# The product x^T k of the last eight tiles in two column halves, with a new order of the work around it

## The chip, the cores and the metric

The kernel runs on one core of a Trainium2 chip. The metric is the device time of one execution in microseconds (us); lower is better. The core has five engines with a queue of instructions each: TensorE (PE; its weight loads are listed as PEld), VectorE (DVE), ScalarE (ACT), GpSimd (POOL) and SyncE (SP), which here issues nearly all DMAs. An engine executes its own queue in order; engines wait for each other and for DMAs through semaphores.

## The reference

Two residual blocks on x (2048 rows of 512, bf16). The first is linear attention with 32 heads of 16 columns after a layernorm, the second a gated mixer; of the second only its outline matters here.

```
xn  = layernorm(x)
q, k, v = xn @ wqkv                      # 512 columns each, 32 heads of 16
phi(t) = where(t > 0, t + 1, exp(t)) + 1e-6
kv  = phi(k)^T v        per head         # 16 x 16
z   = sum over rows of phi(k)            # per head
o   = (phi(q) @ kv) / (phi(q) . z + 1e-6)
h   = x + o @ wo
y   = gelu(layernorm(h) @ w_in);  z1, z2 = halves of y;  z2 = layernorm(z2)
out = h + (z1 * (w_sp @ z2 + b_sp)) @ w_out
```

## The kernel before, in words

The 2048 rows are 16 tiles of 128 rows, in four groups of four tiles. The kernel does not form v. It sums x^T k, a 512 x 512 product of the normalised rows with phi(k), over the 16 tiles in PSUM, and then multiplies this sum by the columns of wqkv that belong to v, head block by head block, masks it to the heads, and multiplies it by wo: the result `mw` turns phi(q), divided by its denominator, straight into o @ wo.

`build` (line 400) writes every operation down once, with `op(engine, cost, function, r=..., w=..., want=..., name=...)`. `Program.schedule` (line 151) then puts the operations of each engine in an order: of those that are possible, it takes on each engine the one with the smallest sum of its planned start and half its `want`. The `want` values that count stand in the list `WANT` (line 359), in the order of the calls of `op` and in tenths of a planned us; they overwrite those of the calls at line 1103. `Program.waits` turns the data dependences into semaphore waits. So the order of each queue, SP's DMAs included, is fixed when the program is built, from planned times, and does not react to real ones.

The operations that the change and the prediction speak of, by name:

- `st`, `ag`, `rs`, `xn` (lines 590 to 668): layernorm of a tile; for tile n, `xn{n}` writes the normalised rows.
- `tx{n}` (line 675, called at 695 and 704): a DMA transpose on SP's queue which writes the transposed tile to `xT`; tiles 2 and 3 are transposed on PE instead, and for k tiles 0 and 1 too.
- `k{n}` (line 758): four matmuls of 512 columns. It needs `tx{n}`. Then `phi` (line 706) makes phi(k): exp by ACT, a `min` by DVE, a `relu` by ACT, and the `sum` by DVE. From tile 4 on, two tiles share these four. `phi` has a second form, used for q: instead of relu and sum, DVE alone does a `max` from PSUM (line 727).
- `xk{n}` (line 768): four matmuls of 512 columns which add the tile's x^T k to the tile `HT` in PSUM, four banks of the eight.
- `q{group}.{f}` (line 860): four matmuls of 512 columns, in pairs, with the group's phi behind them. They need all four transposes of the group.
- `zs`, `zrow`, `ztr`, `zw` (lines 780 to 793): the sum z. `den{group}` (line 873): the denominators of a group; then ACT's `ln` and `rd` (lines 877, 880) give the reciprocals, four DMAs on SP spread them (`sp{group}`, line 886), and DVE multiplies them into phi(q) (`sc{group}.{half}`, line 892).
- `hs{h}.{b}` (lines 801, 804): four copies of `HT` to SBUF, by column half h, one of ACT and one of DVE for each half. `kvT` (line 813), `kvm` (822), `mw` (829) and `mwc` (836, 839) lead from there to `mw`; `kvT1`, `mw1` need half h = 1, `kvT0`, `mw0` half h = 0.
- `o{n}` (lines 905, 912) and `h` (line 924): phi(q) times `mw`, and the residual by DVE. Then the second block: `z2` (968), `z1` (1023), `mix` (1063) and `out` (1083).
- `load` (line 538, the DMA is line 540): `wk`, `wq`, `wv`, `wo`, `win` and the rows of x. `wsp{group}.{st}` (line 1043): 64 DMA transposes from HBM for the mixer, on the same SP queue. `mix` of group 2 waits for all 16 of `wsp2`.

Two lines say how the order is chosen and how x^T k is summed:

```
key = (t + self.WEIGHT * o.want, o.seq)            # WEIGHT = 0.5
i = e.matmul(HT(bank(j)).ap(), lhsT=xn[n, j * P:(j + 1) * P].ap(), rhs=pk[n, :].ap(), ...
```

Of the kernel before, what the change touches and what calls it, by code (L numbers as in the profile page):

```python
# [10 lines left out]
P = 128  # L11
# [81 lines left out]
class Program:  # L93
# [263 lines left out]

UNIT = 0.1
WANT = [
# [37 lines left out]
]  # L397


def build(nc, A_x, A_wqkv, A_wo, B_w_in, B_w_sp, B_b_sp, B_w_out, out):  # L400
# [17 lines left out]
    LN1 = [[0], [1], [2, 3], [4, 5, 6, 7], [8, 9, 10, 11], [12, 13, 14, 15]]  # L418
    LN2 = [[0, 1], [2, 3], [4, 5], [6, 7], [8, 9, 10, 11], [12, 13, 14, 15]]
    ACT_RELU_K = set(range(0, 16))  # L420
    ACT_RELU_Q = set()
    ACT_NORM1 = {5, 7, 9, 11, 13, 15}
    ACT_NORM2 = set()
    ACT_Z = {1, 2, 3, 5, 6, 7, 9, 10, 11, 13, 14, 15}
    UNIT_RES = set()
    FIRST_O = 2

    x_dram, out_dram = A_x[0], out[0]
    g = Program(nc)
# [142 lines left out]
    op("act", (0.1, 1.3), lambda e: e.preload_act_table_set("natural_log_exp_and_others"), want=-40, name="table")  # L572


    HT = Tile(PS, 4)

    def filler(e):
        return e.matmul(HT(bank(0)).ap(), lhsT=nc.const_aps.tensor(1.0, [P, P], BF16),  # L578
                        rhs=nc.const_aps.tensor(1.0, [P, GW], BF16), start=True, stop=True)

    def spin(e):
        for _ in range(SPIN):
            i = filler(e)
        return i
    op("pe", (SPIN * 0.43, SPIN * 0.43 + 0.2), spin, w=[HT()], want=-60, name="spin")
    g.filler = filler


# [148 lines left out]
    for un in UNITS:  # L737
        w = len(un)
        t = Tile(PS, w)
        for ti, n in enumerate(un):  # L740
            lhs = xcT[n].all() if n in LATE else xT[:, n * P:(n + 1) * P]
            for h in range(2):
                rhs = wqkv[2 * h:2 * h + 2, D:2 * D]

                def mm(e, t=t, ti=ti, lhs=lhs, rhs=rhs, h=h):
                    for c in range(2):
                        i = e.matmul(t(bank(ti)).ap(), lhsT=lhs.ap()[:, 2 * h + c, :], rhs=rhs.ap()[:, c, :],
                                     start=(h == 0 and c == 0), stop=(h == 1 and c == 1))
                    return i
                if n in LATE:  # L750
                    op("pe", pe_c(512, 512), mm, r=[xcT[n][2 * h:2 * h + 2, :], rhs, cT[n]()], w=[t()], want=T1(n),
                       name=f"k{n}.{h}")
            if n not in LATE:
                rhs = wqkv[:, D:2 * D]

                def mm(e, t=t, ti=ti, lhs=lhs, rhs=rhs):
                    for c in range(KD):
                        i = e.matmul(t(bank(ti)).ap(), lhsT=lhs.ap()[:, c, :], rhs=rhs.ap()[:, c, :], start=(c == 0),  # L758
                                     stop=(c == KD - 1))
                    return i  # L760
                op("pe", pe_c(*[512] * 4), mm, r=[lhs, rhs], w=[t()], want=T1(n), name=f"k{n}")
        d = pk[un[0]:un[-1] + 1, :]
        src = (lambda t: t(flat).ap()) if w == 2 else (lambda t: t(bank(0)).ap())
        phi(t, w, d, src, False, un[0] in ACT_RELU_K, rs1[un[0]] if un[0] in LATE else None, T1(un[0]) + 1, f"pk{un[0]}")
        for n in un:
            def xk(e, n=n):
                for j in range(KD):
                    i = e.matmul(HT(bank(j)).ap(), lhsT=xn[n, j * P:(j + 1) * P].ap(), rhs=pk[n, :].ap(),  # L768
                                 start=(n == 0), stop=(n == NT - 1))
                return i  # L770
            op("pe", pe_c(*[512] * 4), xk, r=[xn[n, :], pk[n, :]], w=[HT()], want=T1(n) + 3, name=f"xk{n}")


    T0 = T1(NT) + 3
# [21 lines left out]
    for h in range(2):  # L796
        for b in range(2):
            d = hs[2 * b:2 * b + 2, 2 * h * P:2 * (h + 1) * P]
            src = HT(lambda a, b=b, h=h: a[:, 2 * b:2 * b + 2, 2 * h * P:2 * (h + 1) * P])
            if b == 0:  # L800
                op("act", act_c(512), lambda e, d=d, src=src: e.activation(d.ap(), src.ap(), ACT.Copy), r=[HT()], w=[d],
                   want=T0 + 0.5 + h, name=f"hs{h}.0")
            else:
                op("dve", dve_c(512), lambda e, d=d, src=src: e.tensor_copy(d.ap(), src.ap()), r=[HT()], w=[d],
                   want=T0 + 0.5 + h, name=f"hs{h}.1")
    for b in range(2):
        kt, t = Tile(PS), Tile(PS, 2)
# [381 lines left out]
```

## Time and profile before

| | us |
|---|---|
| three runs, median | 241.91 |
| three runs, lowest and highest | 241.69, 244.42 |
| the profiled execution, its own time | 242.55 |
| its span, first to last instruction | 240.8 |
| PE busy in the span | 235.3 |
| DVE, ACT, POOL busy | 127.1, 83.9, 13.9 |

The span is the time between the first and the last instruction that the profiler recorded; the execution's own time is 1.75 us more. A timeline row gives the start, the length in which its merged instructions were busy, the engine (SPq is SP's queue, which issues DMAs), the line, the operation, what it writes and reads, the count, and in brackets how long the engine was idle before. PE's multiplies overlap, so a timeline row of PE ends about 0.17 us after the next one has begun; start to start is the better measure, and the chain of waits shows it. A row "to landing" gives the time from a DMA's issue to its completion.

### The profile page before, as it was taken

Reading aid. Unit: us, or ns where it says so; the run is one execution under the profiler, and the core shown is the slowest. Engines: PE = TensorE matmul, PEld = TensorE weight load, DVE = VectorE, ACT = ScalarE, POOL = GpSimd, SP = SyncE. Lnnn points to the kernel's source line nnn. Section 1 sums busy time; section 2 is a strip of 40 time slices with the busy share of each in tenths; the row PEclk is TensorE's granted clock in tenths of the full one; section 3 lists DMA queues with packets and bytes.
Section 4 is the critical chain, followed back from the end, with each engine's and each line's share of the span. In section 5 each row is a group of like instructions: output and inputs, shape, how many; then the busy total and the mean of one; then the engine's idle time right before and its main releaser. Section 6 shows DMA issues by size and latency. Waiting matters only on the chain.

```text
span 240.8 us, 3056 instructions
## 1 busy us (share of the span) xinstructions
PE 235.3 (98%) x1177; PEld 108.4 (45%) x1199; DVE 127.1 (53%) x269; ACT 83.9 (35%) x132; POOL 13.9 (6%) x33
## 2 busy tenths in 40 slices
PE   8999999999999999999999999999999999999996
PEld 2434445454344544444444444444444444444443
DVE  4999856399999983226222333324333433322443
ACT  4888975566065799994111100000000000000000
POOL 3000000000102160213000000000000000000000
PEclk9999999999999999999999999999999999999999
DMA  6986559632542555444444449463300001000022
GB/s 197 254 224 91 109 114 355 207 112 81 145 125 44 92 107 101 97 88 89 109 92 104 88 92 237 108 89 88 109 0 0 25 22 44 0 3 0 0 87 87
DMA packets 61805, 24.18 MB, mean 100 GB/s; under 512 B 52064, under 2 KB 61152, under 8 KB 61792
## 3 DMA queue, kind: packets, MB, share of 16 engines
q1 hardware_dynamic: 61648, 23.97, 41.3%
q8 instruction: 9, 0.15, 0.3%
q10 hardware_dynamic: 144, 0.03, 0.1%
q14 instruction: 4, 0.03, 0.1%
HBM read 7.47 MB, written 2.10 MB: 40 GB/s over the span
## 4 chain that ended last, share of the span: by engine, by line
PE 87%; DMA 5%; DVE 3%; ACT 2%; SPq 1%; issue 1%; ACTq 0%
PE ps L1063 40%; PE ps L1083 10%; PE ps L968 10%; PE ps L1023 10%; PE ps L768 4%; PE ps L860 4%; DMA xT_pq_z<-k_xn_z 4%; PE ps L905 3%; PE ps L758 3%; PE ps L578 2%; DMA wsp<-e 1%; ACT e L716 1%; SPq L886 1%; DVE xT_pq_z L727 1%; ACT k_xn_z L836 1%
## 5 line engine op out<-in xcount | busy, mean ns | idle before, releaser
L1063 PE MATMUL ps<-wsp,k_xn_z 128*128 128x512 bf16 x328 | 73.6, 379 | 0.4
L1069 DVE TENSOR_TENSOR e<-ps,e 128x512 bf16<-128x512 f32 x28 | 19.4, 692 | 69.2 <-PE ps L1063 69.2
L1063 PEld LDWEIGHTS ps<-wsp,k_xn_z 128*128 128x128 bf16 x336 | 32.8, 98 | 39.8 <-issue 0.4
L1023 PE MATMUL ps<-hT,win 128*128 128x512 bf16 x110 | 26.0, 379 | 0.1
L968 PE MATMUL ps<-win,hT 128*128 128x384 bf16 (+1 forms) x126 | 25.3, 352 | 0.1
L1083 PE MATMUL ps<-wout,xT_pq_z 128*128 128x512 bf16 (+2 forms) x125 | 25.1, 355 | 0.1
L1063 PE MATMUL ps<-wqkv_wsp,k_xn_z 128*128 128x512 bf16 x110 | 24.2, 379 | 0.1
L1028 ACT ACTIVATE xT_pq_z<-ps 128x1024 bf16<-128x1024 f32 x14 | 14.1, 1023 | 25.6 <-PE ps L1023 25.5
L590 DVE BATCH_NORM_STATS2 small<-xh 128x6 f32<-128x512 bf16 x32 | 21.0, 679 | 3.1 <-DMA xh<-in_A_x_dram 3.0
L968 PEld LDWEIGHTS ps<-win,hT 128*128 128x128 bf16 x128 | 12.5, 98 | 12.4
L1083 PEld LDWEIGHTS ps<-wout,xT_pq_z 128*128 128x128 bf16 x126 | 11.8, 98 | 12.7
L1063 PEld LDWEIGHTS ps<-wqkv_wsp,k_xn_z 128*128 128x128 bf16 x112 | 11.0, 98 | 13.2
L1023 PEld LDWEIGHTS ps<-hT,win 128*128 128x128 bf16 x112 | 10.9, 98 | 12.7 <-DVE xh L924 0.3
L1087 DVE TENSOR_TENSOR e<-ps,xh 128x512 bf16<-128x512 f32 (+2 forms) x18 | 11.4, 633 | 9.7 <-PE ps L1083 9.2
L716 ACT ACTIVATE e<-ps 128x1024 bf16<-128x1024 f32 (+1 forms) x16 | 15.4, 973 | 2.4 <-PE ps L860 1.2
L860 PE MATMUL ps<-xT_pq_z,wqkv_wsp 128*128 128x512 bf16 x61 | 15.0, 379 | 0.6 <-DMA xT_pq_z<-k_xn_z 0.5
L768 PE MATMUL ps<-k_xn_z 128*128 128x512 bf16 x63 | 15.2, 379 | 0.2 <-issue 0.2
L975 ACT ACTIVATE k_xn_z<-ps 128x896 bf16<-128x896 f32 x12 | 10.9, 909 | 8.8 <-PE ps L968 8.8
L905 PE MATMUL ps<-k_xn_z,xT_pq_z 128*128 128x512 bf16 x58 | 13.3, 380 | 0.3 <-DVE xT_pq_z L892 0.3
L758 PE MATMUL ps<-wqkv_wsp,xT_pq_z 128*128 128x512 bf16 x55 | 13.2, 379 | 0.2 <-ACT xT_pq_z L701 0.2
L1071 DVE TENSOR_TENSOR xT_pq_z<-xT_pq_z,e 128x512 bf16<-128x512 bf16 x28 | 11.9, 425 | 2.2 <-ACT xT_pq_z L1028 1.3
L979 ACT ACTIVATE e<-k_xn_z 128x896 bf16<-128x896 bf16 x12 | 11.4, 951 | 0.3
(77 smaller groups left out, 169.4 us busy)
## 6 DMA issues: line engine op xcount, KB each, us to landing
wsp<-e SPq DMA_DIRECT2D x16, 128.0 KB
out_dram<-e SPq DMA_DIRECT2D x15, 128.0 KB, 1.7
xh<-in_A_x_dram SPq DMA_DIRECT2D x7, 256.0 KB, 3.8
win<-in_B_w_in_dram SPq DMA_DIRECT2D x1, 1792.0 KB, 7.3
wqkv_wsp<-in_A_wqkv_dram SPq DMA_DIRECT2D x3, 512.0 KB, 7.2
wout<-in_B_w_out_dram SPq DMA_DIRECT2D x1, 896.0 KB, 5.5
wsp<-in_B_w_sp_dram SPq DMA_TRANSPOSE x48, 2.6
wqkv_wsp<-in_A_wo_dram SPq DMA_DIRECT2D x1, 512.0 KB, 5.2
```

Source lines behind the costliest of these rows:

```text
L590: op("dve", (0.577, 0.69), lambda e: e.bn_stats(row[0:6].ap(), src.ap()), r=[src], w=[row[0:6]], want=want, name=name)
L716: first = op("act", act_c(n, ptr=len(pt)), lambda e: e.activation(e_(ev).ap(), src(t), ACT.Exp, scale=sc), r=[t()] + pt, w=[e_()], want=wa ...
L758: i = e.matmul(t(bank(ti)).ap(), lhsT=lhs.ap()[:, c, :], rhs=rhs.ap()[:, c, :], start=(c == 0), stop=(c == KD - 1))
L768: i = e.matmul(HT(bank(j)).ap(), lhsT=xn[n, j * P:(j + 1) * P].ap(), rhs=pk[n, :].ap(), start=(n == 0), stop=(n == NT - 1))
L860: k = e.matmul(t(bank(i)).ap(), lhsT=lhs.ap()[:, c, :], rhs=rhs.ap()[:, c, :], start=(c == 0), stop=(c == KD - 1))
L905: i = e.matmul(t(bank(ti)).ap(), lhsT=l.ap()[:, c, :], rhs=mw[c, :].ap(), start=(c == 0), stop=(c == KD - 1 and not unit))
L968: k = e.matmul(t(bank(i)).ap()[:, 0:b - a], lhsT=l.ap()[:, c, :], rhs=win[c, a:b].ap(), start=(c == 0), stop=(c == KD - 1))
L1023: k = e.matmul(t(bank(i)).ap(), lhsT=l.ap()[:, c, :], rhs=r_.ap()[:, c, :], start=(c == 0), stop=(c == KD - 1))
L1028: op("act", act_c(1024), lambda e: e.activation(d.ap(), t(None if same else flat).ap(), ACT.Gelu_apprx_tanh), r=[t()], w=[d], want=want + ...
L1063: k = e.matmul(t(bank(0)).ap(), lhsT=l.ap()[:, s - a, :], rhs=r_.ap()[:, s - a, :], start=(s == 0), stop=(s == NT - 1))
L1069: op("dve", dve_c(512), lambda e: e.tensor_tensor(gb().ap(), t(bank(0)).ap(), bsp().ap()[:, tg * GW:(tg + 1) * GW], ALU.add), r=[t(), bsp( ...
L1083: k = e.matmul(t(bank(0)).ap()[:, 0:r_.ap().shape[-1]], lhsT=l.ap()[:, fc, :], rhs=r_.ap()[:, fc, :], start=(fc == 0), stop=(fc == KF - 1))
```

## The change

It has four parts.

1. `HT` is two PSUM tiles of two banks, one for each column half of x^T k, instead of one tile of four banks. A bank now holds one column half of two row blocks j.
2. `xk` multiplies 256 columns at a time, so that it has eight matmuls for a tile instead of four. For tiles 0 to 7 the eight are one operation. For tiles 8 to 15 they are two operations of four, `xk{n}.0` and `xk{n}.1`, one for each half, that can stand at different places of PE's queue. The copies `hs0` and `hs1` wait for the last `xk` of their own half alone.
3. In the last q group (q3.0 and q3.2), phi takes its first form: ACT does a `relu` and DVE a `sum`, instead of DVE's `max`.
4. The list `WANT` is new, for all 739 operations (729 before). Read in the order of the calls, it asks for these changes of order:
   - PE, from `xk8` on: `xk8.1 xk8.0 zs0 to zs3 xk9.1 xk10.1 ztr xk11.1 xk12.1 den0 den2 xk9.0 xk13.1 xk14.1 xk15.1 q3.0 q3.1 kvT1 q3.2 q3.3 xk10.0 to xk15.0 mw1 den3 kvT0 q1.0 mw0 q1.1 o2 ...` (before: `xk8 zs0 to zs3 xk9 xk10 ztr q3.2 den2 den0 q3.3 xk11 to xk15 q3.0 q3.1 kvT1 kvT0 q1.0 mw1 mw0 q1.1 den3 o2 ...`).
   - ACT: `ln0 rd0 ln2 hs1.0 rd2`, then exp and relu of q3.0 and of q3.2, `hs0.0 mwc2 mwc3 ln3 rd3 mwc0 pq1.0.exp` (before: `... pq3.0.exp mwc2 mwc0 mwc3 pq1.0.exp ln3 rd3`). DVE follows the same new order.
   - SP: `wsp0.2` goes from behind the eight transposes `tx4` to `tx8` to ahead of them (want 25.3 to 13.2; `tx4` has 14.5). `wv` goes from behind `wo` to ahead of `tx13` and `tx12` (39.6 to 26.3), and `wo` to ahead of `win` (39.0 to 32.0). `wsp2.0` goes from 86.1 to 320.0, which is behind all other `wsp`.
   - The wants of the other operations are close to the order that they had.

```
+    ACT_RELU_Q = {(3, 0), (3, 2)}
+    XK_HALF = range(8, 16)
...
-    HT = Tile(PS, 4)
+    HT = [Tile(PS, 2), Tile(PS, 2)]
...
-            def xk(e, n=n):
+            def xk(e, n, hh):
                 for j in range(KD):
-                    i = e.matmul(HT(bank(j)).ap(), lhsT=xn[n, j * P:(j + 1) * P].ap(), rhs=pk[n, :].ap(),
-                                 start=(n == 0), stop=(n == NT - 1))
+                    for h in hh:
+                        i = e.matmul(HT[h](lambda a: a[:, j // 2, (j % 2) * 2 * P:(j % 2 + 1) * 2 * P]).ap(),
+                                     lhsT=xn[n, j * P:(j + 1) * P].ap(), rhs=pk[n, 2 * h * P:2 * (h + 1) * P].ap(),
+                                     start=(n == 0 and j % 2 == 0), stop=(n == NT - 1 and j % 2 == 1))
                 return i
-            op("pe", pe_c(*[512] * 4), xk, r=[xn[n, :], pk[n, :]], w=[HT()], want=T1(n) + 3, name=f"xk{n}")
+            if n not in XK_HALF:
+                op("pe", pe_c(*[256] * 8), lambda e, n=n, xk=xk: xk(e, n, (0, 1)), r=[xn[n, :], pk[n, :]],
+                   w=[HT[0](), HT[1]()], want=T1(n) + 3, name=f"xk{n}")
+            else:
+                for h in range(2):
+                    op("pe", pe_c(*[256] * 4), lambda e, n=n, h=h, xk=xk: xk(e, n, (h,)),
+                       r=[xn[n, :], pk[n, 2 * h * P:2 * (h + 1) * P]], w=[HT[h]()], want=T1(n) + 3 + h, name=f"xk{n}.{h}")
...
-            src = HT(lambda a, b=b, h=h: a[:, 2 * b:2 * b + 2, 2 * h * P:2 * (h + 1) * P])
+            src = HT[h](lambda a, b=b: a[:, b, :].rearrange("p (j f) -> p j f", j=2))
```

More of the change, by code (lines that the diff above doesn't have):

```diff
@@ L420, in build @@
     ACT_RELU_K = set(range(0, 16))
-    ACT_RELU_Q = set()
+    ACT_RELU_Q = {(3, 0), (3, 2)}
     ACT_NORM1 = {5, 7, 9, 11, 13, 15}
@@ L572, in build @@
     op("act", (0.1, 1.3), lambda e: e.preload_act_table_set("natural_log_exp_and_others"), want=-40, name="table")
-    HT = Tile(PS, 4)
+    HT = [Tile(PS, 2), Tile(PS, 2)]
     def filler(e):
-        return e.matmul(HT(bank(0)).ap(), lhsT=nc.const_aps.tensor(1.0, [P, P], BF16),
+        return e.matmul(HT[0](bank(0)).ap(), lhsT=nc.const_aps.tensor(1.0, [P, P], BF16),
                         rhs=nc.const_aps.tensor(1.0, [P, GW], BF16), start=True, stop=True)
@@ L584, in spin @@
         return i
-    op("pe", (SPIN * 0.43, SPIN * 0.43 + 0.2), spin, w=[HT()], want=-60, name="spin")
+    op("pe", (SPIN * 0.43, SPIN * 0.43 + 0.2), spin, w=[HT[0](), HT[1]()], want=-60, name="spin")
     g.filler = filler
@@ L798, in build @@
             d = hs[2 * b:2 * b + 2, 2 * h * P:2 * (h + 1) * P]
-            src = HT(lambda a, b=b, h=h: a[:, 2 * b:2 * b + 2, 2 * h * P:2 * (h + 1) * P])
+            src = HT[h](lambda a, b=b: a[:, b, :].rearrange("p (j f) -> p j f", j=2))
             if b == 0:
-                op("act", act_c(512), lambda e, d=d, src=src: e.activation(d.ap(), src.ap(), ACT.Copy), r=[HT()], w=[d],
+                op("act", act_c(512), lambda e, d=d, src=src: e.activation(d.ap(), src.ap(), ACT.Copy), r=[HT[h]()], w=[d],
                    want=T0 + 0.5 + h, name=f"hs{h}.0")
             else:
-                op("dve", dve_c(512), lambda e, d=d, src=src: e.tensor_copy(d.ap(), src.ap()), r=[HT()], w=[d],
+                op("dve", dve_c(512), lambda e, d=d, src=src: e.tensor_copy(d.ap(), src.ap()), r=[HT[h]()], w=[d],
                    want=T0 + 0.5 + h, name=f"hs{h}.1")
```

74 rows, old and new, of the table WANT are left out of this document.

## The prediction

> **What bounds the kernel now.** I read the page's first lines, then PE by stretches, then the order of PE, SP and DVE around the places that the change touches.
>
> ```profile
> span 240.8 us, 3056 instructions
> PE 235.3 (98%) x1177; PEld 108.4 (45%) x1199; DVE 127.1 (53%) x269; ACT 83.9 (35%) x132; POOL 13.9 (6%) x33
> PEclk9999999999999999999999999999999999999999
> PE 87%; DMA 5%; DVE 3%; ACT 2%; SPq 1%; issue 1%; ACTq 0%
> ```
>
> PE is busy for 235.3 of 240.8 us at full clock. Only 5.5 us are left in which it does nothing, start and end included. So the change can win little: what idle time of PE it removes. It can lose more, since PE works through its queue in order and every wait that is put in front of a matmul lengthens the span by its whole length, unless a later wait shrinks in turn.
>
> ```profile
> 50.30:54.00 3.70, 3.70 (x33) 2.04 (x31) 3.70 (x8) 2.37 (x4) 0.00 (x0) 1.00 0.25 78
> 58.00:62.00 4.00, 3.72 (x21) 1.51 (x18) 3.39 (x8) 2.54 (x3) 0.96 (x2) 1.00 0.52 176
> ```
>
> The columns are the stretch, its length, then busy time of PE, PEld, DVE, ACT and POOL, the clock and the DMAs. In the stretch 50.3 to 54 both PE and DVE are solid. The one wait around the change is in the last row: 0.28 us of PE.
>
> **Part 1 and 2: halves and banks of their own.** Every matmul of xk becomes two of 256 columns: 16 tiles by 4 more is 64 more matmuls and 64 more weight loads.
>
> ```profile
> 44.39 4.32 PE ps L768 x20
> 50.44 0.89 PE ps L813 x16
> L813 PEld LDWEIGHTS ps<-hT,wqkv_wsp 128*128 128x128 bf16 x16 | 1.0, 98 | 0.2
> ```
>
> In the chain of waits 20 matmuls of 512 columns take 4.32 us, 0.216 each, and 16 of 128 columns 0.89 us, 0.0556 each. Through these two points a matmul costs 0.0021 us and 0.000418 us for a column: 0.109 us at 256 columns, so two halves cost 0.218 where the whole cost 0.216. Times 64: +0.14 us. The weight loads take 98 ns each, but the 16 of L813 go by at 56 ns a matmul, so a load is hidden behind a matmul half as long as the new ones. The upper end is a load that is not hidden: 64 by 98 ns, +6.3 us. I take +0.14, by the row of the 128-column matmuls, the harder case.
>
> The Trainium skill (TensorE: Matmul & The Clock Gate, Back-to-back issue gap) speaks against the change: it gives about 81 ns a matmul at 128 columns and about 131 at 512 for streams of load and matmul, from which I estimate 98 ns at 256, 195 for two halves in place of 131, and 64 by 64 ns, +4.1 us for the sum. This trace does not agree, with 56 and 216 ns for the same two sizes, so the sum stays with the rows.
>
> **Part 3: relu by ACT in the last q group, and the new order from xk8 on.**
>
> The rows are from the timeline, from the groups and, the last five, from the chain of waits.
>
> ```profile
> 40.28 1.67 PE ps L768 x7
> 54.18 1.04 PE L912 MATMUL ps<-k_xn_z,xT_pq_z 128*128 128x512 bf16 x4
> 58.07 3.63 PE L905 MATMUL ps<-k_xn_z,xT_pq_z 128*128 128x512 bf16 x16
> ...
> L722 ACT ACTIVATE e<-ps 128x1024 bf16<-128x1024 f32 x6 | 6.1, 1023 | 2.1 <-PE ps L758 2.1
> L724 DVE TENSOR_TENSOR k_xn_z<-e 128x1024 bf16<-128x1024 bf16 x6 | 4.1, 687 | 1.2 <-ACT e L722 1.1
> L727 DVE SCALAR_TENSOR_TENSOR xT_pq_z<-ps,e 128x1024 bf16<-128x1024 f32 x8 | 9.8, 1222 | 0.1
> ...
> 54.24 0.92 ACT e L716
> 55.75 0.61 ACT e L880
> 58.32 2.88 DMA wsp<-e
> 61.23 0.70 DVE xT_pq_z L892
> 61.98 0.39 PE ps L905
> ```
>
> ACT gains two relu of 1.02 us, DVE trades two max of 1.22 for two sums of 0.69. ACT has room (2.37 of 3.7 us busy above), DVE none. Those five are today's chain into the PE wait: the reciprocal rd3 ends at 56.35, four issues of SP and a landing follow, sc3.0 starts at 61.23 and o12 at 61.98. The 16 matmuls ahead of o12 start at 58.07 and take 0.216 each, to 61.52, so o12 loses some 0.45 us.
>
> With the new queue of PE I add the same pieces from 40.28, where xk9 starts now: halves of four matmuls 0.44 each, a q pair 1.73, kvT 0.45 each. The first halves and ztr, den0 and den2 end near 44.4, q3.0 and q3.1 at 46.2, kvT1 at 46.6, q3.2 and q3.3 at 48.3, the six second halves at 50.9, mw1 at 51.4, den3 at 51.8, kvT0 at 52.2, q1.0, mw0 and q1.1 at 54.4. Today o2 (L912) starts at 54.2: the same work, and as dense. Each new wait has cover: kvT0 needs the copies of half 0, which can start at 51.1 and take 0.6, while mw1 and den3 occupy PE until 51.8; den3 needs the second sum, which I reckon at 51.2 (q3.3 ends 48.3, 0.2 to ACT, exp and relu 0.92 each, the sum 0.69), 0.15 before PE is there; mw0 has q1.0 ahead of it. If the cover of den3 is gone, PE waits by the excess. ACT's queue then gives rd3 near 53.9, 2.4 us earlier, so the four DMAs land near 58.8 and sc3.0 has no DMA to wait for. What is late next is DVE: it is solid from 55 on.
>
> ```profile
> 56.79 1.22 DVE L924 TENSOR_TENSOR xh<-ps,xh 128x1024 bf16<-128x1024 f32 x1
> 59.46 1.19 DVE L924 TENSOR_TENSOR xh<-ps,xh 128x1024 bf16<-128x1024 f32 x1
> ```
>
> ACT's exp for q1.0 and q1.1 comes at 54.6 (54.24 in the chain above), so DVE's h2 starts near 57.2 instead of 56.79, h0 ends near 61.05 and sc3.0 near 61.75. o12 then starts at 61.8 instead of 62.0: -0.2 us. The ends: -0.55, if DVE is not later than now (the 0.45, and 0.1 ahead of o14), and 0, if DVE is 0.2 later than I reckon. den1 may stand ahead of o1 and wait 0.3, which this same slack absorbs.
>
> **Part 4: SP's queue.** Here I find the larger term. wsp0.2 goes ahead of tx4. Nothing else of the eight transposes behind it changes, so each of tx4, tx5, tx6, tx7, tx10, tx11, tx9, tx8 moves one place back.
>
> ```profile
> 14.41 11.10 SPq L675 DMA_TRANSPOSE xT_pq_z<-k_xn_z  x8
> 25.55 2.57 SPq L1043 DMA_TRANSPOSE wsp<-in_B_w_sp_dram  x2
> L675 SPq DMA_TRANSPOSE xT_pq_z<-k_xn_z x8: 1264/1272/1761, 14.4 to 24.2; - x8
> DMA to landing us min/median/max: 2.5/2.8/4.4
> 18.21 1.89 PE L758 MATMUL ps<-wqkv_wsp,xT_pq_z 128*128 128x512 bf16 x8
> 20.80 1.89 PE L758 MATMUL ps<-wqkv_wsp,xT_pq_z 128*128 128x512 bf16 x8
> ```
>
> A place is 1.31 us (1.27 and a short gap): issues at 14.41, 15.72, 17.03, 18.35, 19.8. PE starts k4 at 18.21, k5 at 19.07 (four matmuls later), k6 at 20.80 and k7 at 21.66. Every one of these needs its transpose, and PE does not idle there now. Landings of the second to fifth place, by one window for each issue:
>
> ```profile
> xT_pq_z<-k_xn_z SPq DMA_TRANSPOSE x1, 2.5
> ...
> xT_pq_z<-k_xn_z SPq DMA_TRANSPOSE x1, 3.3
> ...
> q14 instruction: 1, 0.01, 12.6%
> ...
> xT_pq_z<-k_xn_z SPq DMA_TRANSPOSE x1, 4.4
> ...
> q8 instruction: 1, 0.02, 4.6%
> ```
>
> The second place lands at 18.2, in time for k4. The third (issued 17.03, 3.3 us) lands at 20.3; the fourth (18.35, 2.6 us) at 21.0; the fifth (19.8, 4.4 us) at 24.2. The two long ones have an instruction packet in their stretch: 8 KB on q14 at 18.3, 16 KB on q8 at 22.2. tx5 gets the third place, so k5 waits from 19.07 to 20.3: +1.25 us. Its lower end is the shortest landing, 2.5 us: 19.55, +0.5, and then +0.1 more at k7. Behind a k5 at 20.35, xk3 ends at 22.1 and k6 (landed 21.0) at 22.95. k7 needs the fifth place: 22.3 with 2.5 us, nothing more to wait; 24.2 as that place lands today, +1.3 more. Which it is hangs on the 16 KB packet. I take nothing: five of the eight landings are below 3 us, and the packet will not come at the same time.
>
> The Trainium skill (Runtime: NRT & Kernel Launch, Instruction fetch mechanics) says that engines refill instructions in blocks of 16 KiB, 256 instructions, through a DMA queue of their own, and that the cost is mostly hidden. The nine packets of q8 agree in size with it; by "mostly hidden" k5 and k7 would cost the +0.6 of the short landings together, by the landing of 3.3 us they cost +1.25.
>
> wv is moved ahead of tx13 and tx12, wo ahead of win.
>
> ```profile
> 32.05 1.89 PE L758 MATMUL ps<-wqkv_wsp,xT_pq_z 128*128 128x512 bf16 x8
> 39.27 1.32 SPq L540 DMA_DIRECT2D wqkv_wsp<-in_A_wqkv_dram  x1
> wqkv_wsp<-in_A_wqkv_dram SPq DMA_DIRECT2D x3, 512.0 KB, 7.2
> win<-in_B_w_in_dram SPq DMA_DIRECT2D x1, 1792.0 KB, 7.3
> 165.86 2.58 SPq L1043 DMA_TRANSPOSE wqkv_wsp<-in_B_w_sp_dram  x2
> 171.86 4.48 PE L1063 MATMUL ps<-wsp,k_xn_z 128*128 128x512 bf16 x19
> ```
>
> tx12 is then issued near 30.1 (tx8 25.55, wsp0.5 26.85, wv 28.16, tx13 28.8) and lands near 32.6 to 33.1, behind wv's 512 KB (at win's rate 2.1 us). k12 starts at 32.05 now and at 33.3 with the delay of k5, so that delay covers it: 0. If k5 costs only 0.5, k12 takes up to 0.5 instead. Upper end: wv takes the 7.2 us of the crowded start, tx12 lands past 35 and k12 loses 2. wv is needed at 46.2 by kvT1 and is there. wsp2.0 at the end of SP's queue takes the place of today's last transpose (issued near 167.2, landed near 170), and mix of group 2 starts at 171.9: 0.
>
> The sum: +0.14 +1.25 -0.2 = +1.2 us. The profiled execution has 242.55 (span 240.8 and 1.75 around it), 0.64 above the median of the three runs; it would become 243.75, and against the median of 241.91 I predict 243.1 us.
>
> **Rivals.**
> - *Faster: the transposes stay ahead.* The want is only half of what places an operation. If wsp0.2 is still issued behind tx4 to tx8, nothing is lost at k5 and the wait at o12 goes: -0.55 +0.14, 241.5 us. It decides at the issue at 14.41. Against it: when SP is free at 13.2 of the plan, wsp0.2 has 13.2 and half of 13.2, tx4 at least 13.2 and half of 14.5.
> - *The fifth place lands late again:* k7 waits too, 243.1 and 1.3, 244.4 us. For it: 4.4 us today, and the extra matmuls bring the packet earlier, towards that place. A late k12 ends at about the same time.
> - *Short landings:* k5 and k7 cost 0.6 in place of 1.25: 242.5 us. For it: four landings of 2.5 and 2.6.
> - *The weight loads are not hidden* behind 256 columns: +6.3, 249 us. Against it stands L813. The skill's spacing (TensorE: Matmul & The Clock Gate) is a milder form of it.
> - *den3 or kvT0 waits* for the longer ACT chain: each 0.1 us late costs 0.1; 0.5 late gives 243.6 us.
>
> **How the numbers follow.** My forecast (k5 waits about 1.25) 0.40; the fifth place or k12 late 0.23; short landings 0.17; transposes stay ahead 0.12; den3 or kvT0 0.05; loads exposed 0.03. The range 241.5 to 244.5 holds all but the last and the worst of the second; the forecast's own is 242.7 to 243.6. About 2% is what a measurement of this kernel can tell from no change, 4.8 us here: faster needs less than 237.1, and all idle time of PE is 5.5; slower needs more than 246.7, the exposed loads or a pile of late transposes. Faster 0.01, same 0.95, slower 0.04.
>
> **What would show it.** Right: a wait of PE at line 758 near 19 to 20 us for a DMA on xT, no wait of PE at 61.5, a weight load and a 256-column matmul each 0.109 us, sp3's issues near 55 instead of 56.4 (with the delay of k5). Wrong: no such wait at line 758, wsp0.2 behind the transposes, or PE idle between 50 and 54.

## The result, and the profile after

The changed kernel takes 243.87 us (median of 22 runs, 242.87 to 245.71); the kernel before, run beside it, 242.04 us (22 runs, 241.58 to 244.65). The ratio is 1.0063, with an interval of 1.0041 to 1.0085: 1.8 us slower, well outside the noise and well inside 2%. The profiled execution took 244.08 us, 0.2 above its median.

First lines of the page, and the two groups of x^T k:

```profile
span 242.4 us, 3192 instructions
PE 234.8 (97%) x1241; PEld 114.3 (47%) x1263; DVE 125.9 (52%) x269; ACT 85.7 (35%) x134; POOL 13.9 (6%) x33
L770 PE MATMUL ps<-k_xn_z 128*128 128x256 bf16 x128 | 15.8, 273 | 0.0
L770 PEld LDWEIGHTS ps<-k_xn_z 128*128 128x128 bf16 x128 | 12.3, 98 | 3.8 <-issue 0.4
```

PE has 64 more matmuls and 64 more loads, but is busy no longer (234.8 against 235.3). What grew is the time in which it does nothing: 7.6 us against 5.5. PE by stretches shows where; the columns are as in the prediction, the first four rows are of before, the last four of after.

```profile
17.00:23.20 6.20, 6.20 (x31) 2.78 (x30) 6.01 (x14) 5.02 (x7) 0.00 (x0) 1.00 0.70 108
30.80:36.00 5.20, 5.15 (x25) 2.37 (x25) 2.74 (x5) 3.65 (x4) 0.00 (x0) 1.00 0.58 123
52.00:56.00 4.00, 4.00 (x22) 1.67 (x21) 3.97 (x7) 3.31 (x6) 0.00 (x0) 1.00 0.00 0
60.00:66.00 6.00, 5.72 (x27) 2.30 (x26) 5.43 (x11) 0.79 (x1) 0.87 (x2) 1.00 0.52 146
```

```profile
17.00:23.20 6.20, 4.99 (x29) 2.60 (x29) 6.07 (x16) 3.72 (x6) 0.00 (x0) 1.00 0.67 88
30.80:36.00 5.20, 4.82 (x31) 2.84 (x30) 2.77 (x4) 3.18 (x4) 0.00 (x0) 1.00 0.83 171
52.00:56.00 4.00, 3.23 (x24) 1.46 (x23) 3.38 (x6) 3.26 (x7) 0.00 (x0) 1.00 0.02 8
60.00:66.00 6.00, 5.95 (x30) 2.48 (x28) 5.97 (x12) 2.54 (x3) 0.95 (x2) 1.00 0.36 107
```

PE loses 1.21, 0.33 and 0.77 us in three places and gains 0.23 in the fourth. Its timeline rows at the three places (line 759 is k, 770 xk, 882 den, 822 kvT, 914 o):

```profile
17.38 1.96 PE L759 MATMUL ps<-wqkv_wsp,xT_pq_z 128*128 128x512 bf16 x8
19.17 1.04 PE L770 MATMUL ps<-k_xn_z 128*128 128x256 bf16 x8
21.37 1.89 PE L759 MATMUL ps<-wqkv_wsp,xT_pq_z 128*128 128x512 bf16 x7 [1.16 <-DMA xT_pq_z<-k_xn_z]
...
24.82 1.04 PE L770 MATMUL ps<-k_xn_z 128*128 128x256 bf16 x8
25.70 1.89 PE L759 MATMUL ps<-wqkv_wsp,xT_pq_z 128*128 128x512 bf16 x8
...
31.75 1.04 PE L770 MATMUL ps<-k_xn_z 128*128 128x256 bf16 x8
33.11 1.89 PE L759 MATMUL ps<-wqkv_wsp,xT_pq_z 128*128 128x512 bf16 x8 [0.33 <-ACT e L717]
...
52.98 0.40 PE L882 MATMUL ps<-xT_pq_z,small 128*32 128x512 bf16 x4 [0.52 <-DVE xT_pq_z L725]
53.59 0.62 PE L822 MATMUL ps<-hT,wqkv_wsp 128*128 128x128 bf16 x8 [0.20 <-DVE hT L813]
...
60.08 7.24 PE L914 MATMUL ps<-k_xn_z,xT_pq_z 128*128 128x512 bf16 x31
```

Eight matmuls of 256 columns take 0.88 us where nothing is waited for (24.82 to 25.70). So k6, at 21.37, is 1.32 us later than 19.17 and 0.88 would allow, and k12, at 33.11, is 0.48 later than 31.75 and 0.88; den3 and kvT0 are 0.68 and 0.28 late (two matmuls of mw1 from 51.87 and four of den3, at 0.43 and 0.33); 0.2 of these 0.96 is there without a wait too, as the trace of a_rd_own below has it (51.78, 52.30, 52.75), so the wait costs 0.75. The o matmuls run from 60.08 on without a gap: the wait ahead of o12 is gone.

**First place.** The chain of waits before k6, and a window around one issue of SP:

```profile
17.04 4.20 DMA xT_pq_z<-k_xn_z
21.24 0.14 issue
21.37 0.59 PE ps L759 x2
```

```profile
q8 instruction: 1, 0.02, 20.5%
xT_pq_z<-k_xn_z SPq DMA_TRANSPOSE x2, 3.9
```

tx6 was issued at 17.04 and landed 4.20 us later. The 16 KB instruction packet on q8, which before came at 22.2, now starts at 18.4 and takes 1.3 us, inside that landing (the two transposes in the window of 18.2 to 18.6 are tx6 and tx7, 4.2 and 3.6 us). SP's row for the eight transposes:

```profile
14.42 11.59 SPq L676 DMA_TRANSPOSE xT_pq_z<-k_xn_z  x8
```

tx4 is issued at 14.42 as before, although wsp0.2 is now ahead of it: in this execution SP's queue ran a place earlier, and k4 started 0.8 us earlier. So tx5 was issued at 15.73, as the second transpose was before, and k5 did not wait.

**Second place.** The row of k12 blames ACT, but the exp that ends then (that of q2.2) touches nothing that k12 reads or writes: k12 needs tx12, `wk` and the two PSUM banks of k8 and k9. One window over SP's issues at 27.9 to 28.1, another at 29.1 to 29.4:

```profile
wqkv_wsp<-in_A_wqkv_dram SPq DMA_DIRECT2D x1, 512.0 KB, 4.6
xT_pq_z<-k_xn_z SPq DMA_TRANSPOSE x1, 4.5
...
xT_pq_z<-k_xn_z SPq DMA_TRANSPOSE x2, 4.1
```

tx13, right behind wv, took 4.5 us and tx12 3.7 (4.1 is the median with tx13's), where the same two took 2.5 each before. tx12, issued at 29.24, landed at 32.98, and PE started 0.13 us later, the same step as after tx6; a_wsp_back and a_spin, below, have the same 0.13, and there the row names the DMA.

**Third place.** The chain that ended last, by time, from den0 to kvT0 (line 886 is `ln`, 889 `rd`, 895 the spread's issues, 723 relu, 725 the sum, 813 the copy hs0):

```profile
43.12 0.36 PE ps L882 x4
...
43.50 0.67 ACT ps L886
...
44.19 0.60 ACT e L889
...
46.33 0.61 SPq L895
...
46.98 4.11 DMA wsp<-e
...
51.11 1.03 ACT e L723
...
52.24 0.69 DVE xT_pq_z L725
52.93 0.61 DVE hT L813
...
53.59 0.62 PE ps L822 x8
```

The relu of q3.2 does not wait for PE's q3.3. It waits for the DMAs that spread the reciprocals of group 0: relu's result goes to a buffer of a pool of three (`RB`) that relu and `rd` share, and the one whose turn it is was filled by rd0 and is read by those DMAs until 51.09 (46.98 and 4.11). Relu, the sum, the copy hs0 and so den3 and kvT0 come late by this. Sharing alone does not make the wait: it also takes a spread that lands as late as this one did, 4.11 us after its last issue.

### The profile page after: what moved, and what is told of

The parts are those of the page before. It is cut to its first block, busy times and chain, and to the rows that moved or that the text cites. A ratio compares the mean times of both kernels' runs of the same rounds, so it can differ in the third digit from the quotient of the medians.

```text
span 242.4 us, 3192 instructions
## 1 busy us (share of the span) xinstructions
PE 234.8 (97%) x1241; PEld 114.3 (47%) x1263; DVE 125.9 (52%) x269; ACT 85.7 (35%) x134; POOL 13.9 (6%) x33
## 4 chain that ended last, share of the span: by engine, by line
PE 82%; ACT 6%; DVE 5%; DMA 5%; SPq 1%; issue 1%; DVEq 0%
PE ps L1072 40%; PE ps L977 10%; PE ps L1092 10%; PE ps L1032 10%; PE ps L914 5%; PE ps L759 2%; ACT e L717 2%; DVE small L591 2%; ACT e L723 2%; DMA xT_pq_z<-k_xn_z 2%; DMA wsp<-e 2%; PE ps L770 1%; PE ps L869 1%; DMA xh<-in_A_x_dram 1%; ACT k_xn_z L626 1%
## 5 line engine op out<-in xcount | busy, mean ns | idle before, releaser
L977 PE MATMUL ps<-win,hT 128*128 128x512 bf16 (+1 forms) x127 | 25.3, 352 | 0.1
L1072 PEld LDWEIGHTS ps<-wqkv_wsp,k_xn_z 128*128 128x128 bf16 x112 | 11.0, 98 | 13.2
L717 ACT ACTIVATE e<-ps 128x1024 bf16<-128x1024 f32 (+1 forms) x16 | 15.5, 974 | 4.1 <-PE ps L759 2.9
L770 PE MATMUL ps<-k_xn_z 128*128 128x256 bf16 x128 | 15.8, 273 | 0.0
L759 PE MATMUL ps<-wqkv_wsp,xT_pq_z 128*128 128x512 bf16 x55 | 13.2, 379 | 1.7 <-DMA xT_pq_z<-k_xn_z 1.2
L869 PE MATMUL ps<-xT_pq_z,wqkv_wsp 128*128 128x512 bf16 x60 | 14.4, 379 | 0.2
L770 PEld LDWEIGHTS ps<-k_xn_z 128*128 128x128 bf16 x128 | 12.3, 98 | 3.8 <-issue 0.4
```

Of the source, the lines that this page charges most:

```text
L717: first = op("act", act_c(n, ptr=len(pt)), lambda e: e.activation(e_(ev).ap(), src(t), ACT.Exp, scale=sc), r=[t()] + pt, w=[e_()], want=wa ...
L770: i = e.matmul(HT[h](lambda a: a[:, j // 2, (j % 2) * 2 * P:(j % 2 + 1) * 2 * P]).ap(), lhsT=xn[n, j * P:(j + 1) * P].ap(), rhs=pk[n, 2 * ...
L869: k = e.matmul(t(bank(i)).ap(), lhsT=lhs.ap()[:, c, :], rhs=rhs.ap()[:, c, :], start=(c == 0), stop=(c == KD - 1))
L977: k = e.matmul(t(bank(i)).ap()[:, 0:b - a], lhsT=l.ap()[:, c, :], rhs=win[c, a:b].ap(), start=(c == 0), stop=(c == KD - 1))
L1072: k = e.matmul(t(bank(0)).ap(), lhsT=l.ap()[:, s - a, :], rhs=r_.ap()[:, s - a, :], start=(s == 0), stop=(s == NT - 1))
```

## The experiments

The theory: all of the loss is these three waits, each made by an order or a buffer and none by the time of the smaller matmuls; removing them brings the kernel back to the time of before, and only then can the removed wait at o12 show. The rivals: the halves themselves cost time (64 more loads and matmuls), ACT's relu costs by its work, or the place of the instruction packet alone makes the loss.

Kernels whose names begin with b_ are the kernel before with one part of the change, those with a_ the changed kernel with one part undone. Where a queue is changed, the program is scheduled once, the named operations are moved in one engine's order, and it is scheduled again in that order; all the rest stays. A move is written as engine, operation, and the operation that it is put ahead of. Times are medians, with the ratio to the kernel before on the same chip and its interval. The start of the kernel differs by up to 1 us from one execution to the next, so where traces are compared, the time from k4 to the end is given as well, the page's span less the start of k4's row: 222.6 us before (240.8 less 18.21) and 225.0 after (242.4 less 17.38).

**wsp0.2 alone, in the kernel before.** b_wsp_fwd:

```
+MOVES = [("sp", "wsp0.2", "tx4")]
-    g.schedule()
+    g.reorder(MOVES)
```

> The kernel before with one move on SP's queue: wsp0.2 ahead of tx4, everything else as before. Place theory: k5, k6 or k7 wait for their transposes, which come 1.3 us later; 0.5 to 1.3 us more, 242.6 to 243.3 us. Packet theory: without the added PE instructions the packet stays near 22 us, where k7 or the transposes behind it are under way; k5 to k7 lose the slack of 0.5 to 0.8 but little more, 242.1 to 242.7 us.

Measured: 243.09 us, 1.0043 (1.0022 to 1.0064), +1.25 us on 241.84. From k4 on 223.6 us. The first row is from the chain of waits, the others are PE's timeline:

```profile
16.09 3.43 DMA xT_pq_z<-k_xn_z
...
17.59 1.03 PE L775 MATMUL ps<-wqkv_wsp,xT_pq_z 128*128 128x512 bf16 x4
...
19.57 1.04 PE L775 MATMUL ps<-wqkv_wsp,xT_pq_z 128*128 128x512 bf16 x4 [0.96 <-DMA xT_pq_z<-k_xn_z]
...
62.47 1.90 PE L922 MATMUL ps<-k_xn_z,xT_pq_z 128*128 128x512 bf16 x8 [0.28 <-DVE xT_pq_z L909]
```

Here it is k5 that waits for tx5, issued at 16.09, and the wait at o12 stays; the 16 KB packet comes at 21.1, after tx5 has landed. From k4 to k6 the trace is 1.13 us longer than before (3.72 against 2.59), so it agrees with the medians. One transpose moved ahead of eight others in SP's queue costs two thirds of the whole loss by itself.

**The halves alone, in the kernel before.** b_halves: the two tiles of `HT` and the 256-column matmuls for all 16 tiles, one operation each, with the list `WANT` and the phi of before. Against the changed kernel that is, beside the list:

```
-    ACT_RELU_Q = {(3, 0), (3, 2)}
+    ACT_RELU_Q = set()
...
-    XK_HALF = range(8, 16)
+    XK_HALF = ()
```

> The kernel before with x^T k in two column halves for all 16 tiles, both halves in one operation, in the order of before everywhere, without the relu of the last q group. Matmuls cost 0.109 us at 256 columns: +0.14 us in all, 242.2 us, if nothing else happens. Packet theory: 32 more PE instructions by tile 3 bring the packet from 22.2 to about 18.4 us, where it delays tx6 or tx7 to about 21.2, and k6 or k7 waits 0.2 to 0.5: 242.4 to 242.7 us. Loads that are not hidden behind 256 columns would give 248 us.

Measured: 242.2 us, 1.0012 (0.9985 to 1.0039), so +0.3 us with an interval from -0.4 to +0.9. Its profiled execution took 244.68 us, 2.5 above its median, so no size of the change is read from its trace. The halves are not the loss: loads in the open (+6.3) and the estimate of +4.1 are excluded. That execution shows something else, though. The packet comes at 18.9, tx6 takes 4.9 us, and k6 waits 1.0 us, without any new order: the halves by themselves bring the packet onto the transposes. By the median of the twelve runs this costs little in most executions, or does not come about in them. A second wait of 1.0 us in that trace, at mw1, is not explained here.

**The packet moved, in the changed kernel.** a_spin gives PE more instructions ahead of the tiles: each 512-column filler at the start becomes four of 128 columns, which is 24 more matmuls with a load each (the page lists 47 more instructions).

```
-        for _ in range(SPIN):
-            i = filler(e)
+        for _ in range(4 * SPIN):
+            i = e.matmul(HT[0](lambda a: a[:, 0, 0:P]).ap(), lhsT=nc.const_aps.tensor(1.0, [P, P], BF16),
+                         rhs=nc.const_aps.tensor(1.0, [P, P], BF16), start=True, stop=True)
```

> The changed kernel with the eight 512-column matmuls of the warm-up at the start replaced by 32 of 128 columns: the same PE time, 48 more PE instructions ahead of everything else, SP's queue untouched. Packet theory: the 16 KB packet of q8 moves some 48 instructions forward, from 18.4 to about 13 us, away from tx6, which lands near 19.6; k6's wait goes and the time falls by about 1.1 to 242.8 us. Place theory: instruction packets do not matter, tx6 lands near 21.2 again, 243.9 us.

Measured: 243.85 us, 1.0069 (1.0043 to 1.0095). From k4 on 224.1 us. A window of 14.5 to 15.5, one of 16 to 18, and PE:

```profile
q8 instruction: 1, 0.02, 6.3%
...
xT_pq_z<-k_xn_z SPq DMA_TRANSPOSE x3, 2.5
```

```profile
18.31 1.73 PE L760 MATMUL ps<-wqkv_wsp,xT_pq_z 128*128 128x512 bf16 x7 [0.58 <-DVE k_xn_z L726]
32.61 1.89 PE L760 MATMUL ps<-wqkv_wsp,xT_pq_z 128*128 128x512 bf16 x8 [0.45 <-DMA xT_pq_z<-k_xn_z]
52.76 0.40 PE L883 MATMUL ps<-xT_pq_z,small 128*32 128x512 bf16 x4 [0.79 <-DVE xT_pq_z L726]
```

The packet came at 15.0, the transposes of 16 to 18 took 2.5 us and k6 had nothing to wait for. So the packet is what made tx6 late. But the time did not move, against the 242.8 us of the packet theory. The packet now meets tx4, which takes 3.3 us and lands at 17.95, and k4's row, in which one of eight matmuls is missing, starts at 18.31 after a wait that the time from k4 on leaves out; k12 and den3 wait as before. The run moves the packet and does not remove it; with tx6 in time the loss stays.

**One repair at a time, in the changed kernel.** a_wsp_back returns wsp0.2, a_wv_back returns wv, a_rd_own gives rd a buffer of its own, a_no_relu gives q3.0 and q3.2 DVE's max again. The move of bsp in a_rd_own leaves SP's order that of the changed kernel, as the two traces show.

```
a_wsp_back: MOVES = [("sp", "wsp0.2", "wsp0.5")]
a_wv_back:  MOVES = [("sp", "wv", "wo")]
a_rd_own:   MOVES = [("sp", "bsp", "th1")]
-        b, rw = Tile(PS), Tile(RB)
+        b, rw = Tile(PS), View(s_wout, 0, [NG, GW], BF16)[gq, :]
a_no_relu:
-    ACT_RELU_Q = {(3, 0), (3, 2)}
+    ACT_RELU_Q = set()
```

> The changed kernel with one move on SP's queue: wsp0.2 goes back behind tx8. Place theory (tx6 is late because each transpose stands one place further back): k6's wait of 1.2 us at 21.4 goes, the time falls by about 1.2 to 242.7 us. Packet theory (tx6 is late because PE's 16 KB instruction packet falls at 18.4 us while it is under way): the packet still falls at 18.4 and hits whichever transpose is under way, now tx7, which then lands near 21.2; k6 does not wait, k7 waits some 0.3 to 0.5 us, time 243.0 to 243.2. If neither holds, 243.9.

> The changed kernel with wv behind tx15 on SP's queue, just ahead of wo, instead of ahead of tx13 and tx12. The trace of after shows tx12 landing at 33.0 and k12 starting at 33.1, 0.33 us after PE was free. Theory (wv's 512 KB hold up the four transposes): tx12 lands near 31.3, k12 does not wait, -0.3 us, 243.6 us; kvT1 still finds wv landed by 40. Rival (k12 waits for ACT's exp, as the waits view has it): 243.9 us.

> The changed kernel with the reciprocals rd in a buffer of their own (in the still empty space of wout) instead of sharing the three relu buffers; the order of all queues as in the changed kernel. Buffer theory (the second relu of the last q group waits for the four DMAs that spread rd0, since it gets the buffer of rd0, and den3 waits for that relu's sum): the relu starts near 50.4 instead of 51.1 (counted in the trace of after), PE's 0.5 us wait ahead of den3 goes, 243.3 us. Rival (ACT's and DVE's own work is what makes den3 late): the wait stays within 0.2 us, 243.8 us.

> The changed kernel with the last q group's phi as before (max by DVE, no relu by ACT), the order of all else as in the changed kernel. Buffer theory: without the relu there is no wait for a relu buffer; the max of q3.2 ends near 52.2 instead of the sum at 52.9, den3 waits less by 0.5, time 243.4 us. If DVE, which gets 1.06 us more work, is the limit for kvT0 and o2 instead, the gain is given back: 243.9 us or more.

| | median us | ratio | from k4 on |
|---|---|---|---|
| a_wsp_back | 243.67 | 1.0061 (1.0037 to 1.0084) | 224.2 |
| a_wv_back | 243.52 | 1.0067 (1.0041 to 1.0093) | 224.2 |
| a_rd_own | 243.93 | 1.0070 (1.0044 to 1.0097) | 224.2 |
| a_no_relu | 243.97 | 1.0072 (1.0048 to 1.0095) | 224.2 |

No single repair moves the ratio. The rows of PE in a_wsp_back and, behind them, in a_wv_back show why for two of them:

```profile
21.81 1.04 PE L776 MATMUL ps<-wqkv_wsp,xT_pq_z 128*128 128x512 bf16 x4 [0.44 <-DMA xT_pq_z<-k_xn_z]
33.40 1.89 PE L776 MATMUL ps<-wqkv_wsp,xT_pq_z 128*128 128x512 bf16 x8 [1.03 <-DMA xT_pq_z<-k_xn_z]
```

```profile
21.72 1.89 PE L776 MATMUL ps<-wqkv_wsp,xT_pq_z 128*128 128x512 bf16 x7 [1.32 <-DVE small L608]
```

With wsp0.2 back, k6 has its transpose in time, the packet falls on tx7 and k7 waits 0.44, and PE then reaches k12 earlier and waits there 1.03 for a tx12 that is no sooner: 1.47 in the two places, where the changed kernel waits 1.16 and 0.33, which is 1.49. With wv back k12 waits no more, but tx6 has the packet in its landing again, k6 waits 1.32 (tx6 landed at 21.58, the waits view names DVE), more than in the changed kernel. So k12 takes over what is repaired at k6. The reverse is not shown, and the order of SP's queue speaks against it: wv stands behind tx6 and cannot make it later, so the longer wait at k6 is a difference of the execution. The medians of these two, 0.2 and 0.35 us below that of the changed kernel, are within what their intervals allow, and so is no gain at all; a_wsp_back does not reach the 243.0 to 243.2 of its packet theory, although k7 waits as that theory said.

In a_rd_own and a_no_relu den3 and kvT0 start without a wait that the waits view lists. But so they do in a_wsp_back and a_wv_back, where relu still shares its buffers with rd. The relu of q3.2 in these two, a_wsp_back first:

```profile
50.66 1.02 ACT L740 ACTIVATE e<-ps 128x1024 bf16<-128x1024 f32 x1
50.23 1.02 ACT L740 ACTIVATE e<-ps 128x1024 bf16<-128x1024 f32 x1
```

It follows its exp without a wait: the spread, last issued at 47.27 and 46.84, had landed within 3.4 us. So the third wait is not in every execution. The shared buffer makes it possible, and the landing of the spread decides; why that landing takes 4.11 us in the changed kernel's trace and at most 3.4 in these two stays open (a 16 KB packet starts during it in all three). That the buffer of its own does what it is for can be seen in a_rd_own: there the last completion of the spread comes at 51.81, and relu starts at 50.28 all the same. All four traces are 0.8 us shorter from k4 on than that of the changed kernel, nearly all of it at den3 and kvT0, and still no ratio is clearly lower; a_rd_own and a_no_relu come out at the times of their rivals (243.8 and 243.9), not at those of the buffer theory. With intervals of some 0.6 us each way on every ratio a gain of half a microsecond is not excluded; what this repair is worth alone stays open.

**The repairs together.** a_sp makes the two moves on SP, a_all these and the buffer of rd. a_best puts wsp0.2 further back, behind wsp0.5, four transposes, wv, wo and win (ahead of wsp0.3), so that these are issued one place earlier, and is otherwise a_all; a_best_max is a_best with DVE's max in place of the buffer. before_again is the kernel before, once more in the same place.

```
a_sp:       MOVES = [("sp", "wsp0.2", "wsp0.5"), ("sp", "wv", "wo")]
a_all:      a_sp, and a_rd_own
a_best:     MOVES = [("sp", "wsp0.2", "wsp0.3"), ("sp", "wv", "wo"), ("sp", "bsp", "th1")], rd as in a_rd_own
a_best_max: MOVES = [("sp", "wsp0.2", "wsp0.3"), ("sp", "wv", "wo")], ACT_RELU_Q = set()
```

> The changed kernel with the two repairs of SP's queue alone: wsp0.2 behind tx8, wv behind tx15; the reciprocals share the relu buffers as in the changed kernel. Theory of two waits that cover each other (each alone gave 0.2 to 0.35 us because the other's wait takes its place; together they free PE up to den3): 242.9 to 243.3 us, with a wait of PE of 1 us or more ahead of den3, because the relu still waits for the DMAs of rd0, which do not come earlier. Rival (the buffer does not matter, the two SP moves are all): 242.1 us as with all three repairs.

> The changed kernel with three repairs: wsp0.2 behind tx8, wv behind tx15, the reciprocals in a buffer of their own. If the three causes add up, 243.9 less 0.8 to 1.2, 0.3 and 0.5: 241.9 to 242.3 us, level with the kernel before. If they cover each other (a wait that is removed uncovers the next), 242.6 to 243.2 us.

> The kernel with all three repairs, in which wsp0.2 goes further back, behind win, so that tx13 and tx12 are issued one place earlier. The trace of the three repairs still shows k12 waiting 0.4 us for tx12 (landed at 31.8). If that is the last wait between k4 and the mixer, the time falls by 0.4 to 241.7 us, 0.1 to 0.4 below the kernel before; if another wait takes its place, 242.1 us.

> The changed kernel with SP's queue as in the version before this one, but the last q group's phi as in the kernel before (max by DVE, no relu on ACT), so that no relu buffer is needed. Buffer theory: as fast as with a buffer of its own for the reciprocals, within 0.3 us: 241.7 to 242.0 us. If the relu by ACT is worth something on its own (DVE is full from 55 us on), 242.3 us or more.

> The kernel before once more, for a second profile: how far the first transposes and the instruction packets move from one execution to the next. If the start alone differs, k4 begins between 17.2 and 18.2 us and everything behind it is shifted by as much; PE's wait ahead of o12 is 0.4 to 0.5 us again.

| | median us | ratio | from k4 on |
|---|---|---|---|
| a_sp | 242.92 | 1.0036 (1.0006 to 1.0065) | 223.1 |
| a_all | 242.12 | 1.0008 (0.9990 to 1.0026) | 222.8 |
| a_best | 241.93 | 0.9989 (0.9961 to 1.0017) | 223.2 |
| a_best_max | 241.84 | 0.9991 (0.9963 to 1.0019) | 222.3 |
| before_again | 242.21 (one run) | | 222.6 |

With all three repairs the kernel is level with the one before: the intervals of the changed kernel, 1.0063 (1.0041 to 1.0085), and of a_all do not overlap. How the gain divides is not shown. By the medians both moves together take back nearly half of the loss and the buffer the rest, but the intervals of these two steps overlap; by the traces, from k4 on, the moves take back 1.9 us (225.0 to 223.1) and the buffer 0.3. a_all and a_best_max came at the times that were expected of them, a_best between its two. In a_sp the relu of q3.2 still waits for the spread, and den3 and kvT0 for what follows, but only some 0.4 us together, where 1 us or more ahead of den3 was expected; first ACT's row, then two of PE.

```profile
49.78 1.02 ACT L740 ACTIVATE e<-ps 128x1024 bf16<-128x1024 f32 x1 [0.26 <-DMA wsp<-e]
```

```profile
32.15 1.89 PE L776 MATMUL ps<-wqkv_wsp,xT_pq_z 128*128 128x512 bf16 x8 [0.20 <-DMA xT_pq_z<-k_xn_z]
...
52.25 0.62 PE L839 MATMUL ps<-hT,wqkv_wsp 128*128 128x128 bf16 x8 [0.20 <-DVE hT L830]
```

a_best and a_best_max are faster than the changed kernel by some 1.8 us, going by the ratios, and equal to the kernel before: both intervals contain 1. Their traces also show what chance is left in it. In a_best's profiled execution (243.06, the longest of its twelve runs) the packet fell on tx7, which took 4.2 us, and k7 waited; in a_best_max's (241.55) it fell on a transpose with slack, and from k4 to o14 the waits view lists no wait of PE at all. A row of each:

```profile
22.43 1.04 PE L776 MATMUL ps<-wqkv_wsp,xT_pq_z 128*128 128x512 bf16 x4 [0.71 <-DMA xT_pq_z<-k_xn_z]
```

```profile
57.56 7.24 PE L931 MATMUL ps<-k_xn_z,xT_pq_z 128*128 128x512 bf16 x32
```

The second row is the gain that the change makes possible: 32 matmuls of o with no wait at o12, worth 0.45 us in the trace of before (61.98 against 58.07 and 16 times 0.216). It is not as steady as was expected of before_again: there o12 starts at 61.53, 0.30 us later than 57.77 and 16 times 0.216 would allow, and the waits view lists no wait. Against it stands the way from k4 to o2, which without a wait takes 0.23 us longer than before (36.20 us in a_best_max, 35.97 in both traces of before), the smaller matmuls and their order together. From k4 on a_best_max is 0.3 us shorter than both traces of before, but 0.3 us is less than the medians can show.

## Why the prediction was right or wrong

The forecast was +1.2 us for the median, measured are +1.8. The time lies in the range on record, above the forecast's own (242.7 to 243.6), because two of its rivals, a late k12 and a late den3, came true beside a wait of the forecast's size. That this wait has the forecast's size in the profiled execution, 1.32 us for 1.25, is luck: it is at k6 and not at k5, and it comes of the packet in tx6's landing, not of the long landing that I had read for the third place. Of the signs on record, o12 and sp3 (issued from 54.86) came as said; the wait near 19 to 20 us did not, and one sign of being wrong did: PE idle between 50 and 54.

From k4 on the profiled executions differ by 2.4 us. Start to start this is 1.32 at k6, 0.48 at k12, 0.75 at den3 and kvT0 and some 0.3 between these places, for the matmuls and their order, less 0.41 from o2 to the second block (11.37 us before, 10.96 after). The changed one had started k4 0.8 us earlier, which is why the spans differ by 1.6 only; the start varies by itself, as a_best_max (17.48) and a_best (18.10) show, which have the same work in the same order ahead of k4, or before_again (17.92) and before (18.21).

- *64 more matmuls, +0.14.* Right as far as it can be seen: +0.3 in b_halves, with 0.14 in its interval (the traces, with the new order, have 0.23 from k4 to o2). Eight matmuls of 256 columns take 0.88 us in the trace, 0.11 each with its load, as the line through the two sizes said. By the Trainium skill's spacing (TensorE: Matmul & The Clock Gate, Back-to-back issue gap) my estimate was 0.098, near to this, but its 131 ns for 512 columns is far from the 0.216 here, and it is that figure from which the +4.1 came.
- *k5 waits, +1.25.* The mechanism is right for the move alone: wsp0.2 costs 1.25 us in the kernel before, at k5, with a landing of 3.43 us where I had 3.3. In the changed kernel's own trace this step failed. The transposes stood one place further back, but the queue ran a place earlier, and k5 found tx5 landed. It is k6 that waits, 1.32 us, with another packet. I took the long landing of the third place as a property of the place, from the 8 KB packet on q14 at 18.3, and counted on the 16 KB packet not coming at the same time as the fifth. In fact the 32 more instructions of PE ahead of k6 (four matmuls and four loads for each of four tiles) brought the 16 KB packet from 22.2 to 18.4, onto the transpose issued at 17.04. That is the time of what I had called the third place, but with SP's queue a place earlier it is tx6 that stands there, and k6 that waits. That the packet would come earlier stood in the rival; where it would land did not.
- *k7, 0.* Right: k7 follows k6 without a wait.
- *wv, 0.* Failed. That tx12 landed when I had said (32.6 to 33.1; it was 32.98) is luck: it was issued at 29.24 and not near 30.1, and took 3.74 us behind wv where I had allowed 2.5 to 3.0. PE came to k12 at 32.63 and not at 33.3, so the cover was too short by 0.48 with its start. And the place is worth more than that: as a_wsp_back shows, k12 takes over what is repaired at k6, up to 1.03.
- *den3 and kvT0, 0.* Failed. I priced the chain to the second sum by the durations of ACT and DVE, and gave den3 a cover of 0.15. (The pieces as I named them end at 51.0; with relu at 1.02 and the steps between they end at 51.2, and a_rd_own agrees: its sum ends 2.9 us after q3.3, as 51.2 is 2.9 after 48.3.) What the relu writes to was not priced: a buffer of a pool shared with rd, free only when DMAs of another group have landed. That put relu 0.64 us late and PE 0.75 in this trace. a_rd_own, where relu has not to wait for that landing, has no such wait; a_wsp_back and a_wv_back, where the landing came sooner, have none either.
- *o12, -0.2.* Too small: the wait is gone whole, -0.41 from o2 on, within the bound of -0.55. I had DVE as the next to be late there; a_best_max, where den3 and kvT0 are in time, has no wait at o12 either, so it is not.
- *wsp2.0, 0.* Right: mix of group 2 has no wait worth a row. The line is from the page of after:

```profile
L1072 PE MATMUL ps<-wqkv_wsp,k_xn_z 128*128 128x512 bf16 x110 | 24.2, 379 | 0.1
```

The sum's error is thus two terms set to nothing, 0.48 and 0.75 us in this trace, for cover that was an estimate of 0.15 in one case and depended on another wait in the other. A third error does not show in the sum: in this trace the wait that it has at k5 is another one, at k6.

## What to carry to other kernels

When an engine is busy for 98% of its span, look less at what a reordering wins than at what each moved DMA stands in front of: here, in b_wsp_fwd, 1.3 us on SP's queue became 1.25 us of PE. When an operation is given to another engine, price its output buffer too, by who read that buffer last and when that read ends. And undo suspects in combination, not only one at a time: a later wait on an in-order queue can take over what an earlier one gives back, as k12 did for k6, and three repairs of which none moved the ratio alone were together worth the whole loss. A wait that one trace shows need not be in the next execution, so read the place in several traces before pricing it.

## What the runs showed of the hardware

- A DMA transpose whose landing overlaps a 16 KB instruction packet took 3.0 to 4.9 us in place of 2.5 in these traces: tx6 4.20 after, tx7 4.2 in a_best, the fifth place 4.4 before, tx6 4.9 in b_halves. With the packet elsewhere the same transposes take 2.5 (a_spin).
- The packet's time follows the number of PE's instructions: it came between 21.1 and 22.2 in three traces with the matmuls of before, between 18.3 and 20.3 in ten with 32 more instructions ahead of k6 (18.9 in b_halves, which changes nothing else on PE), and at 15.0 with 48 more still (a_spin). What spreads it within the ten is not shown.
- Transposes behind a plain load of 512 KB land late: tx13 and tx12 took 4.5 and 3.7 us behind wv and 2.5 each without it (a_wv_back).
